# The first loads of a gated mixing kernel laid side by side, and its first two products by turns

## The chip, the cores and the metric

The kernel runs on one core of one Trainium2 chip. The metric is the device time of one execution in microseconds (us), the median over several runs. The engines are TensorE (PE, matrix multiplication, with PEld for its weight loads), VectorE (DVE), ScalarE (ACT), GpSimd (POOL) and SyncE (SP). Here SP issues nearly all loads from HBM, and POOL the stores of intermediate results.

## The reference

One input x of 2048 x 512 goes two ways, and a gate of x mixes the two:

```python
g = sigmoid((x * gate_w).sum(-1))
a = Re(DFT_seq @ (x @ DFT_hid))                     # 2048 x 512
b = (silu(x @ w1) * (x @ w3)) @ w2                  # w1, w3: 512 x 1376, w2: 1376 x 512
out = g * a + (1 - g) * b
```

All of it is float32. The change touches only the start of `x @ w1` and `x @ w3`.

## The kernel before, in words

**Arithmetic.** PE multiplies fp32r operands, a rounded form of float32. To keep float32 accuracy each operand is split into a high part (rounded) and a low part (the rest), and a product takes three matmuls: high times high, low times high, high times low. `high` (line 107) rounds on ACT, `low` (line 110) subtracts on DVE, and `split` does both.

**Blocks.** The products are done by a Strassen-like scheme on 2 x 2 blocks. Of x transposed the blocks are B11, B12, B21 and B22 (each 128 partitions x 1024 columns, 512 KB; a "half" g of 1024 tokens has four of them), and sums of them called T1 to T4 (line 203). The weights w1 and w3 come in 11 chunks of 128 columns; a chunk is 128 x 1024 and holds A11, A12, A22 and A21 with 256 columns each. Seven products make one item, that is one chunk with one half of x.

**Order.** The order of the instructions is the program's own (`manual_schedule`, line 401): every engine runs its instructions in the order in which the code emits them, and waits on semaphores for what it reads and for buffers to come free. The first item (chunk 0, half 0) is written out by hand in lines 402 to 502 and done without the seven-product scheme: eight plain block products into four PSUM tiles, C00, C10, C01, C11, each `half(...)` being six matmuls (two parts r of the contraction, three matmuls each). From line 474 on the usual scheme begins: `prod1` and `prod2` make two products of a chunk ahead (X and Y), and `gate_up(n)` (line 338) does the rest of item n.

**The start.** SP first loads A11 alone (line 402, 128 rows of 1024 bytes), then B11 (line 403, 128 rows of 4096 bytes), then the other three blocks of chunk 0 (line 410, rows of 3072 bytes), then B21, B12, B22, then chunks 1, 2 and 3 (lines 411 to 415). DVE clears a tile `warm` (line 405), and PE multiplies it WARM = 11 times by itself in bf16 (lines 407 and 408), whose results nobody reads. Then come A11's split, B11's split in pieces (lines 444 to 447), the product C00 of A11 with B11, A21's split and the product C10 of A21 with B11, and so on. Chunk 4's load (line 461) reuses the place of chunk 0.

**Places.** The four x blocks lie in F32 places `F4`, of which there are four at that time; T2, T3 and T4 are written over B11, B12 and B21 (lines 466, 494, 501). At line 509 the four places are freed, and the blocks of half 1 are loaded into them. The split parts of half 1 have a large tile of their own in pool `xo1`, written only from item 2 on.

Of the kernel before, what the change touches and what calls it, by code (L numbers as in the profile page):

```python
# [7 lines left out]
F32 = mybir.dt.float32  # L8
F32R = mybir.dt.float32r
# [3 lines left out]
P = 128  # L13
# [4 lines left out]
TB = 512  # L18
# [5 lines left out]
NP2 = (NC + 1) // 2  # L24
WARM = 11
LOOK = 3
# [6 lines left out]
def fnet_swiglu_gate_kernel(  # L33
    ctx: ExitStack,
    tc: tile.TileContext,
    xn: bass.AP,
    xt: bass.AP,
    cc: bass.AP,
    dd: bass.AP,
# [67 lines left out]
    def high(hi, src):  # L107
        nc.scalar.activation(hi, src, AF.Copy)  # L108

    def low(hi, lo, src):  # L110
        nc.vector.tensor_sub(lo, src, hi.bitcast(F32))  # L111

    def split(hi, lo, src):
        high(hi, src)
        low(hi, lo, src)
# [79 lines left out]
    def load_xo(g, k):  # L195

        if g not in XO:
            XO[g] = (xo1 if g else xo0).tile([P, 2, 7, 2, 512], F32R, tag="xo", name=f"xo{g}")
        ST[g, k] = wide(f"xs{g}_{k}")
        nc.sync.dma_start(ST[g, k], xt[g, XRAW.index(k)])  # L200
# [20 lines left out]
    def load_w(w, lo=0, hi=4):  # L221
        if lo == 0:
            WS[w] = f4_a.tile([P, 4, 256], F32, tag=f"f4_{4 + w % (LOOK + 1)}", name=f"ws{w}")
        nc.sync.dma_start(WS[w][:, lo:hi].rearrange("p a n -> p (a n)"),  # L224
                          w13[SETS[w], :, lo * 256 : hi * 256])
# [7 lines left out]
    def wa_parts(w, lo, hi):  # L233
        return (*(flat(WA[w][:, h, lo:hi]) for h in range(2)), flat(WS[w][:, lo:hi]))
# [166 lines left out]
    ctx.enter_context(tc.manual_schedule())  # L401
    load_w(0, 0, 1)
    load_xo(0, "B11")
    warm = s1p.tile([P, 1024], mybir.dt.bfloat16, tag="s1", name="warm")[:, :512]
    nc.vector.memset(warm, 0.0)
    wps = bank(7, "wps")
    for n in range(WARM):
        nc.tensor.matmul(wps, warm[:, :P], warm, start=True, stop=True)
    nc.scalar.activation(act0, warm[:, :24], AF.Silu)
    load_w(0, 1, 4)  # L410
    for k in ("B21", "B12", "B22"):
        load_xo(0, k)
# [8 lines left out]

    def half(i, j, w, x, start):


        wp = lambda h, sl: a21[:, h, sl] if w is None else WA[0][:, h, w, sl]
        xp = lambda q, h: b12[:, h, q * 512 : (q + 1) * 512] if x is None else XO[0][:, h, x, q, :]
        for r in range(2):
            sl = slice(r * P, (r + 1) * P)
            for n, (u, v) in enumerate(((0, 0), (1, 0), (0, 1))):
                nc.tensor.matmul(C[i, j], wp(u, sl), xp(r, v), start=start and r == n == 0,  # L430
                                 stop=not start and r == 1 and n == 2)
# [9 lines left out]
    new_wa(0)  # L441
    split(*wa_parts(0, 0, 1))

    hi, lo, src = xo_half("B11", 0)
    high(hi[:, :256], src[:, :256])
    nc.vector.tensor_copy(hi[:, 256:], src[:, 256:])
    low(hi, lo, src)
    split(*xo_half("B11", 1))
    half(0, 0, 0, 0, True)
    split(a21[:, 0], a21[:, 1], WS[0][:, 3])  # L450
    half(1, 0, None, 0, True)
    split(*wa_parts(0, 1, 3))
    for q in range(2):
        split(*xo_half("B21", q))
    half(0, 0, 1, 1, False)
# [4 lines left out]
    half(0, 1, 0, None, True)  # L460
    WS.pop(0)
    load_w(4)
    sum_xo(0, "T1", t1)
    half(1, 1, None, None, True)
    nc.vector.tensor_mul(h0[:, :512], s1, C[1, 0])
    store_h(0, 0, h0[:, :512])
    sum_xo(0, "T2", ST[0, "B11"])
    half(0, 1, 1, 2, False)
    for w in (1, 2):
        new_wa(w)  # L470
        split(*wa_parts(w, 0, 3))
    half(1, 1, 2, 2, False)
# [35 lines left out]
    do(ahead, 1, lambda: split_xo(0, "T4"))  # L508
    do(second, 1, free, *(ST[0, b] for b in ("B11", "B21", "B12", "B22")))
    do(second, 1, sum_g, 2, y2)  # L510
# [505 lines left out]
```

## Time and profile before

| what | us |
|---|---|
| median of 3 runs | 709.98 (709.84 to 710.0) |
| the profiled execution | 710.08 |
| its span in the profile | 708.3 |
| PE busy in the span | 702.8 |
| DVE busy | 605.1 |
| ACT busy | 369.4 |

The profile is of one execution. The span runs from its first to its last instruction in the trace; the rest of its time lies outside of that. In the rows below, times are from the span's start. A row of the timeline gives the start, the duration, the engine, the line, the operation, what is written and read, how many instructions are merged in it and, in brackets, the idle time ahead of it with what ended it. A row of the groups gives the busy time and the mean duration in ns, and behind the next bar the idle time ahead of the group's instructions. A row of the DMA issues ends with the time from issue to landing. Durations of matmuls overlap, so the distance from one start to the next is their real cost.

### The profile page before, as it was taken

How to read it: one execution, taken by the hardware profiler on the slowest of the kernel's cores; microseconds unless marked ns; L12 is line 12 of the kernel's file. 1: busy time of each engine (PE TensorE's matmuls, PEld its weight loads, DVE VectorE, ACT ScalarE, POOL GpSimd, SP SyncE). 2: the span in 40 equal slices, each digit the busy share in tenths (PEclk: the TensorE clock that was granted, in tenths of full speed). 3: DMA queues.
4: the chain of work that ended last, by engine and by line, in shares of the span. 5: the costliest groups of instructions: out<-in, count | busy, mean ns of one | idle time of the engine just before them, and what ended most of it. 6: DMA issues, size and time to landing. Idle time of an engine off the chain costs nothing.

```text
span 708.3 us, 8597 instructions
## 1 busy us (share of the span) xinstructions
PE 702.8 (99%) x3089; PEld 578.6 (82%) x3089; DVE 605.1 (85%) x735; ACT 369.4 (52%) x479; POOL 64.0 (9%) x118
## 2 busy tenths in 40 slices
PE   9999999999999999999999999999999999999997
PEld 6888888888888888888888888888888888888886
DVE  7989988787679999877999589969997896898985
ACT  6666555655446754454554553544455455455451
POOL 0011111211110000000110001100110000000000
PEclk9999999999999999999999999999999999999999
DMA  7676546499997566712596238914999971773932
GB/s 281 222 270 231 214 183 255 178 319 356 417 412 270 212 210 233 282 60 89 179 358 250 90 129 298 359 60 179 384 418 415 356 274 54 298 281 139 321 120 89
DMA packets 45403, 172.54 MB, mean 244 GB/s; under 512 B 5296, under 2 KB 5424, under 8 KB 41520
## 3 DMA queue, kind: packets, MB, share of 16 engines
q1 hardware_dynamic: 32464, 118.50, 45.6%
q0 software_dynamic: 12608, 52.97, 18.8%
q8 instruction: 24, 0.39, 0.2%
q10 hardware_dynamic: 288, 0.52, 0.2%
q14 instruction: 19, 0.16, 0.1%
HBM read 114.82 MB, written 57.16 MB: 243 GB/s over the span
## 4 chain that ended last, share of the span: by engine, by line
PE 99%; DMA 1%; DVE 0%; ACT 0%; SPq 0%; issue 0%
PE P L119 69%; PE X L119 16%; PE Z L119 8%; PE Y L119 4%; PE C L430 2%; DMA xs_B<-xt 1%; DVE zc L809 0%; ACT xo L108 0%; SPq L224 0%
## 5 line engine op out<-in xcount | busy, mean ns | idle before, releaser
L119 PE MATMUL P<-zo,a 128*128 128x512 f32 x1344 | 305.5, 389 | 0.0
L119 PEld LDWEIGHTS P<-zo,a 128*128 128x128 f32 x1344 | 252.0, 188 | 53.4 <-DVE zo L111 1.1
L108 ACT ACTIVATE zo<-B 128x1024 fp32r<-128x1024 f32 (+1 forms) x182 | 189.2, 1045 | 184.5 <-PE P L119 96.9
L111 DVE TENSOR_TENSOR zo<-B,zo 128x1024 fp32r<-128x1024 f32 (+1 forms) x182 | 217.4, 1202 | 48.3 <-ACT zo L108 47.5
L119 PE MATMUL P<-zo,H 128*128 128x512 f32 x468 | 106.2, 389 | 0.0
L119 PEld LDWEIGHTS P<-zo,H 128*128 128x128 f32 x468 | 87.8, 188 | 18.2
L667 DVE TENSOR_TENSOR B<-B,B 128x1024 f32<-128x1024 f32 (+1 forms) x78 | 92.7, 1188 | 0.1
L119 PE MATMUL X<-xo,wb 128*128 128x512 f32 x378 | 92.7, 389 | 0.0
L119 PEld LDWEIGHTS X<-xo,wb 128*128 128x128 f32 x378 | 70.9, 188 | 14.7
L119 PE MATMUL P<-zo,Y 128*128 128x512 f32 x336 | 76.3, 389 | 0.0
L119 PEld LDWEIGHTS P<-zo,Y 128*128 128x128 f32 x336 | 63.1, 188 | 13.1
L327 POOL DMA_DIRECT2D hsp<-h x42 | 23.0, 548 | 127.4 <-DVE h L381 75.4
L119 PE MATMUL X<-xo,wa 128*128 128x512 f32 x126 | 32.0, 389 | 0.0
L119 PE MATMUL Y<-xo,wa 128*128 128x512 f32 x126 | 32.0, 389 | 0.0
L119 PE MATMUL Z<-xo,wb 128*128 128x512 f32 x126 | 32.0, 389 | 0.0
L119 PE MATMUL Z<-xo,wa 128*128 128x512 f32 x126 | 32.0, 389 | 0.0
L670 DVE TENSOR_TENSOR B<-B,B 128x1024 f32<-128x1024 f32 x26 | 31.6, 1217 | 0.0
L884 ACT ACTIVATE zu<-P 128x512 f32<-128x512 f32 x32 | 19.1, 598 | 20.3 <-PE P L119 20.3
L375 DVE TENSOR_TENSOR u<-u,X 128x512 f32<-128x512 f32 x21 | 14.4, 687 | 15.9 <-PE X L119 15.9
L119 PEld LDWEIGHTS Y<-xo,wa 128*128 128x128 f32 x126 | 23.6, 188 | 4.9
L119 PEld LDWEIGHTS X<-xo,wa 128*128 128x128 f32 x126 | 23.6, 188 | 4.9
L119 PEld LDWEIGHTS Z<-xo,wa 128*128 128x128 f32 x126 | 23.6, 188 | 4.9
(135 smaller groups left out, 549.6 us busy)
## 6 DMA issues: line engine op xcount, KB each, us to landing
B<-cc SPq DMA_DIRECT2D x64, 512.0 KB, 6.0
hsp<-h POOLq DMA_DIRECT2D x42, 256.0 KB, 3.6
B<-hsp SPq DMA_DIRECT2D x20, 512.0 KB, 10.4
wbsp<-wb POOLq DMA_DIRECT2D x8, 1024.0 KB, 4.2
wb<-wbsp SPq DMA_DIRECT2D x8, 1024.0 KB, 8.0
B<-zsp SPq DMA_DIRECT2D x16, 512.0 KB, 7.7
H<-w2sp SPq DMA_DIRECT2D x6, 1024.0 KB, 9.4
ws<-w SPq DMA_DIRECT2D x11, 512.0 KB, 4.4
```

The source lines that it names most:

```text
L108: nc.scalar.activation(hi, src, AF.Copy)
L111: nc.vector.tensor_sub(lo, src, hi.bitcast(F32))
L119: nc.tensor.matmul(ps, u, v, start=first and n == 0, stop=last and n == 2, skip_group_check=chain)
L327: nc.gpsimd.dma_start(hsp[g, b + k, j // 2, :, j % 2 * 512 : (j % 2 + 1) * 512], h)
L375: nc.vector.tensor_add(u4, u4, x)
L430: nc.tensor.matmul(C[i, j], wp(u, sl), xp(r, v), start=start and r == n == 0, stop=not start and r == 1 and n == 2)
L667: nc.vector.tensor_add(t, t, RAW[blk, b, q][:, :n])
L670: nc.vector.tensor_sub(t, RAW[blk, "B12", q], t)
L884: nc.scalar.activation(U[name][:, r], ps[r], AF.Copy)
```

## The change

The host lays out one more input, `first`, of three rows of 128 x 1024: [A11, A21, left half of B11], [right half of B11, left half of B21], [right half of B21, A12, A22]. A left or right half has 512 columns. The kernel loads the three with one DMA each, all with rows of 4096 bytes, into the place of the tile that later holds half 1's split parts; B11 and B21 are views of it, and T2 and T4 are written there too. Chunk 0 has no load of its own any more. The warm-up multiplies a constant tile of ones that the program's preamble sets, 9 times instead of 11, and DVE's clearing goes. The left half of B11 is rounded by DVE in one cast of 512 columns (before: half by ACT, half by DVE). The two products of B11 are done by turns, so that each matmul comes about when its split part does; A12 and A22 are split apart, between the halves of B21; chunk 1 is split ahead of the sum T2. Chunk 4's load doesn't wait for chunk 0's place. F4's places are used by two x blocks instead of four, and so the loads of B11 and B21 of half 1 have places that were never used.

```diff
-WARM = 11
+WARM = 9
...
-    load_w(0, 0, 1)
-    load_xo(0, "B11")
-    warm = s1p.tile([P, 1024], mybir.dt.bfloat16, tag="s1", name="warm")[:, :512]
-    nc.vector.memset(warm, 0.0)
+    tf = xo1.tile([P, 2, 7, 2, 512], F32, tag="xo", name="first")
+    tf = tf.rearrange("p h o q n -> p (h o q n)")[:, : 3 * 1024]
+    XO[0] = xo0.tile([P, 2, 7, 2, 512], F32R, tag="xo", name="xo0")
+    for i in range(3):
+        nc.sync.dma_start(tf[:, i * 1024 : (i + 1) * 1024], first[i])
+    ST[0, "B11"], ST[0, "B21"] = tf[:, 512:1536], tf[:, 1536:2560]
+    RAW0 = {k: tf[:, n : n + 256] for k, n in (("A11", 0), ("A21", 256), ("A12", 2560), ("A22", 2816))}
+    warm = nc.const_aps.tensor(1.0, [P, 512], mybir.dt.bfloat16)
...
-    load_w(0, 1, 4)
-    for k in ("B21", "B12", "B22"):
+    for k in ("B12", "B22"):
         load_xo(0, k)
...
-    def half(i, j, w, x, start):
+    def half(i, j, w, x, start, some=None):
...
+                if some is not None and (r, n) not in some:
+                    continue
...
-    split(*wa_parts(0, 0, 1))
+    w_parts = lambda i, k: (WA[0][:, 0, i], WA[0][:, 1, i], RAW0[k])
     hi, lo, src = xo_half("B11", 0)
-    high(hi[:, :256], src[:, :256])
-    nc.vector.tensor_copy(hi[:, 256:], src[:, 256:])
+    nc.vector.tensor_copy(hi, src)
+    split(*w_parts(0, "A11"))
     low(hi, lo, src)
+    split(a21[:, 0], a21[:, 1], RAW0["A21"])
     split(*xo_half("B11", 1))
-    half(0, 0, 0, 0, True)
-    split(a21[:, 0], a21[:, 1], WS[0][:, 3])
-    half(1, 0, None, 0, True)
-    split(*wa_parts(0, 1, 3))
-    for q in range(2):
-        split(*xo_half("B21", q))
+    for i, some in ((0, ((0, 0), (0, 1))), (1, ((0, 0),)), (0, ((0, 2),)), (1, ((0, 1), (0, 2))),
+                    (0, ((1, 0), (1, 1))), (1, ((1, 0), (1, 1))), (0, ((1, 2),)), (1, ((1, 2),))):
+        half(i, 0, None if i else 0, 0, True, some)
+    split(*xo_half("B21", 0))
+    split(*w_parts(1, "A12"))
+    split(*xo_half("B21", 1))
+    split(*w_parts(2, "A22"))
     half(0, 0, 1, 1, False)
...
-    WS.pop(0)
     load_w(4)
...
+    new_wa(1)
+    split(*wa_parts(1, 0, 3))
     sum_xo(0, "T2", ST[0, "B11"])
     half(0, 1, 1, 2, False)
-    for w in (1, 2):
-        new_wa(w)
-        split(*wa_parts(w, 0, 3))
+    new_wa(2)
+    split(*wa_parts(2, 0, 3))
     half(1, 1, 2, 2, False)
...
-    do(second, 1, free, *(ST[0, b] for b in ("B11", "B21", "B12", "B22")))
+    do(second, 1, free, *(ST[0, b] for b in ("B12", "B22")))
...
+    a11, a12, a22, a21 = arrays["w13"][0].reshape(P, 4, 2 * P).transpose(1, 0, 2)
+    v = np.concatenate([a11, a21, arrays["xt"][0, 1], arrays["xt"][0, 2], a12, a22], 1)
+    arrays["first"] = v.reshape(P, 3, 2 * TB).transpose(1, 0, 2)
```

In the pairs (r, n) of the new loop, r is the part of the contraction (0 takes the left half of B11, 1 the right) and n the matmul of the three: 0 high times high, 1 weights' low part times x's high part, 2 weights' high part times x's low part.

More of the change, by code (lines that the diff above doesn't have):

```diff
@@ L37, in fnet_swiglu_gate_kernel @@
     xt: bass.AP,
+    first: bass.AP,
     cc: bass.AP,
@@ L998 @@
         "xt": np.stack(xq, 1).reshape(2, 4, P, 2 * TB),
+        "first": None,
         "cc": np.stack(cb, 1).reshape(NTB, 4, NG // 2, P, 2 * TB),
```

## The prediction

> **What bounds the kernel now.** I read the page first, then the groups by line for PE, then the chain of waits of the first 8 us, then the timeline and the DMA issues of the first 40 us.
>
> ```profile
> span 708.3 us, 8597 instructions
> ...
> PE 702.8 (99%) x3089; PEld 578.6 (82%) x3089; DVE 605.1 (85%) x735; ACT 369.4 (52%) x479; POOL 64.0 (9%) x118
> ...
> PE 99%; DMA 1%; DVE 0%; ACT 0%; SPq 0%; issue 0%
> ```
>
> TensorE (PE in the rows; DVE is VectorE, ACT ScalarE, SP the engine that issues the loads) is the bound and the chain that ends last is 99% PE. The groups by line, with idle time in the last column:
>
> ```profile
> L119 PE MATMUL P<-zo,a 128*128 128x512 f32 x1344 | 305.5, 389 | 0.0
> ```
>
> Every matmul group from line 119 has 0.0 idle like this first one: once the stream runs it doesn't stop. So the change can save only what lies before it: the first real matmul may start sooner, and the first groups may wait less. The first 8 us of the chain, and PE's first rows:
>
> ```profile
> 1.19 3.93 DMA xs_B<-xt
> ...
> 5.15 0.42 ACT xo L108
> ...
> 5.62 2.38 PE C L430 x8
> ```
> ```profile
> 0.74 0.40 SPq L224 DMA_DIRECT2D ws<-w  x1
> 0.86 0.27 DVE L405 MEMSET warm<- 128x256 uint32 x1 [0.86 <-PEq L1006]
> 1.19 3.89 PE L408 MATMUL wps<-warm 128*128 128x512 bf16 x11 [1.19 <-DVE warm L405]
> 5.62 1.92 PE L430 MATMUL C<-xo,wa 128*128 128x512 f32 x6 [0.54 <-ACT xo L108]
> 8.76 2.88 PE L430 MATMUL C<-xo,wa 128*128 128x512 f32 x12
> 11.48 1.52 PE L430 MATMUL C<-b,wa 128*128 128x512 f32 x6
> ```
>
> B11 lands at 1.19 + 3.93 = 5.12, ACT rounds its first piece, and the first real matmul starts at 5.62; PE stood idle 0.54 us after the warm-ups. The 12 matmuls from 8.76 to 11.48 take 2.72 us, a pitch of 0.227 us. The first 12 (the two products of B11) take 8.76 - 5.62 = 3.14, so 0.42 us more than 2.72, in waits for splits. What the change does not touch follows as it is, moved as a whole.
>
> **The change, part by part.**
>
> *First load.* Before, SP issues A11 (128 KB) at 0.74, B11 (512 KB) at 1.19, the rest of chunk 0 (384 KB) at 1.66, then B21, B12, B22. After, the first issue at 0.74 is a 512 KB load that holds A11, A21 and the left half of B11, and two more such loads follow. When does it land? SP's issues in the timeline, and the time from issue to landing, the rows in the order A11, B11, and then the four of the timeline rows:
>
> ```profile
> 2.13 0.43 SPq L200 DMA_DIRECT2D xs_B<-xt  x1
> ...
> 3.08 0.46 SPq L200 DMA_DIRECT2D xs_B<-xt  x1
> ...
> 27.51 0.33 SPq L200 DMA_DIRECT2D xs_B<-xt  x1
> ...
> 29.82 0.33 SPq L200 DMA_DIRECT2D xs_B<-xt  x1
> ```
> ```profile
> ws<-w SPq DMA_DIRECT2D x1, 128.0 KB, 2.4
> ...
> xs_B<-xt SPq DMA_DIRECT2D x1, 512.0 KB, 3.9
> ...
> xs_B<-xt SPq DMA_DIRECT2D x1, 512.0 KB, 5.2
> ...
> xs_B<-xt SPq DMA_DIRECT2D x1, 512.0 KB, 6.8
> ...
> xs_B<-xt SPq DMA_DIRECT2D x1, 512.0 KB, 3.3
> ...
> xs_B<-xt SPq DMA_DIRECT2D x1, 512.0 KB, 3.2
> ```
>
> B21 landed at 2.13 + 5.2 = 7.33 and B22 at 3.08 + 6.8 = 9.88, with B12 between, so 1.27 us for each 512 KB once the queue is full (413 GB/s). The last two are loads of the second half, of the same shape, that found nothing of SP's queue ahead of them: 3.3 and 3.2 us. B11's 3.9 has A11 ahead. From below: 0.74 + 3.2 = 3.94. From A11: 2.4 us for 128 KB plus 384 KB at 413 GB/s (0.95 us) is 3.35, landing at 4.09. From above, B11's 3.93: landing at 4.67. I take **4.10**, nearest to A11's own row at the same time with nothing ahead. It compares with 5.12. The other two loads follow at 1.27 us each: 5.4 and 6.6. B22 stands behind the same 2560 KB as before, so it gains only the idle stretch around A11: I take 9.4 against 9.88.
>
> *From landing to the first matmul.* The splits, by shape:
>
> ```profile
> L111 DVE TENSOR_TENSOR xo<-xs_B,xo 128x512 fp32r<-128x512 f32 x4 | 2.6, 688 | 0.4 <-ACT xo L108 0.4
> L111 DVE TENSOR_TENSOR a<-ws,a 128x256 fp32r<-128x256 f32 x1 | 0.4, 418 | 0.0
> L446 DVE CAST xo<-xs_B 128x256 fp32r<-128x256 f32 x1 | 0.3, 295 | 1.1 <-DMA xs_B<-xt 1.1
> ```
> ```profile
> L108 ACT ACTIVATE xo<-xs_B 128x512 fp32r<-128x512 f32 x3 | 1.8, 621 | 0.3 <-DMA xs_B<-xt 0.3
> L108 ACT ACTIVATE xo<-xs_B 128x1024 fp32r<-128x1024 f32 x4 | 4.2, 1062 | 2.7 <-DVE xs_B L207 2.4 <-DMA xs_B<-xt 0.2
> ```
>
> The first matmul needs A11's high part (ACT, 0.42, as before) and the high part of all 512 columns of B11's left half, now one DVE cast. A cast of 512 columns isn't in the trace: at least 0.295 (the 256 cast), at most 0.59 (twice it). I take 0.44, about ACT's 0.42, so it costs at most 0.17 more. First matmul at 4.10 + 0.03 + 0.44 + 0.05 = **4.62**, which is 1.00 earlier than 5.62.
>
> *Two products by turns.* PE's order is C00 twice, C10, C00, C10 twice, then likewise for the right half; DVE's is cast, A11 low (256), B11 left low (512), A21 low (256), B11 right low (512). In the trace DVE starts of 256 lie 0.33 apart, of 512 0.60. A11 low ends 5.02, so matmul 2 is at 5.07 (0.22 late); matmul 3 at 5.30; B11 left low ends 5.61, matmul 4 at 5.66 (0.13 late); A21 low ends 5.95, matmul 5 at 6.00 (0.11 late). Matmul 7, due 6.45, needs the right half's high part: 5.4 + 0.62 + 0.08 = 6.1, in time. Matmul 11, due 7.36, needs its low part: 6.8. So the 12th ends its turn at 7.81, 3.19 us after 4.62: the waits are 0.47 where they were 0.42, which **loses 0.05**. The B21 products want A12 low at about 8.0; A12 lands at 6.6, and ACT 0.42 and DVE's queue put it at 7.7. In time.
>
> *Warm-ups.* The memset (0.27) goes, so PE starts about 0.86 instead of 1.19, and 9 remain instead of 11.
>
> ```profile
> 2.02 0.15 PEld L408 LDWEIGHTS <-warm 128*128 128x128 bf16 x1 [0.28 <-issue]
> 2.45 0.15 PEld L408 LDWEIGHTS <-warm 128*128 128x128 bf16 x1 [0.28 <-issue]
> ...
> 4.06 0.53 PEld L408 LDWEIGHTS <-warm 128*128 128x128 bf16 x3 [0.18 <-issue]
> ```
>
> Their pitch was 0.43 us until about 4.1 and half of that after: full rate came 2.9 us after the first one. Nine from 0.86 end between 4.4 (rate doubles at 4.1) and 4.7 (it doesn't): by 4.62 or 0.08 late. I cost them at nothing. [...]
>
> *Vector queue behind it.* DVE becomes the question, since it is full there:
>
> ```profile
> 12.00:14.00 2.00, 2.00 (x11) 1.65 (x10) 2.00 (x4) 1.08 (x2) 0.00 (x0) 1.00 0.98 401
> ...
> 20.00:25.00 5.00, 5.00 (x24) 4.14 (x23) 5.00 (x6) 3.77 (x6) 1.09 (x2) 1.00 0.46 161
> ```
>
> The third time of a row is DVE: 2.00 of 2 us and 5.00 of 5 us, and the two stretches between the rows are as full. What opens this, and what PE waits for behind it:
>
> ```profile
> 11.04 1.23 DVE L111 TENSOR_TENSOR xo<-xs_B,xo 128x1024 fp32r<-128x1024 f32 x1
> ...
> 16.79 1.22 DVE L111 TENSOR_TENSOR xo<-xs_B,xo 128x1024 fp32r<-128x1024 f32 x1
> ...
> 25.35 0.96 DVE L111 TENSOR_TENSOR wa<-ws,wa 128x768 fp32r<-128x768 f32 x1 [0.33 <-ACT wa L108]
> 32.99 1.23 DVE L111 TENSOR_TENSOR wb<-wu,wb 128x1024 fp32r<-128x1024 f32 x1 [0.53 <-ACT wb L108]
> 33.24 2.88 PE L119 MATMUL X<-xo,wb 128*128 128x512 f32 x12
> 36.05 0.95 DVE L111 TENSOR_TENSOR wa<-ws,wa 128x768 fp32r<-128x768 f32 x1
> 37.32 1.52 PE L119 MATMUL X<-xo,wa 128*128 128x512 f32 x6
> ```
>
> The first row, B22's low part, waits for B22 (9.88) and ACT's 1.06; with B22 at 9.4 it starts at 10.55, 0.5 earlier and not 0.95. The second row, T2's low part, is 5.75 us behind the first. After the change the low part of chunk 1 stands ahead of the sum T2 and no longer behind it, where the low parts of chunks 1 and 2 covered ACT's rounding of T2 (1.06): 10.55, then T1 (1.15), h0 (1.13), chunk 1 (0.6 + 0.9) and T2 (1.2) end at 15.55, ACT at 16.64, and T2's low part starts at 16.68, only 0.1 earlier. At 33.24 the seventh matmul (34.60) starts chunk 2's second set; its second (34.83) needs the low part that ends 34.22: 0.6 us to spare. At 37.32 the second (37.55) needs what ends 37.00: 0.55 to spare. PE moves up 0.95. DVE moves up 0.1 at T2's low part and, since the 0.33 us wait at 25.35 is for an ACT step that follows PE, gets back to 0.3 to 0.5 from there. So these two spots are short by 0.95 - 0.4 - 0.55 = 0 to 0.1. I take **0.10 lost**. Behind 40 us PE needs 8.16 us for the 36 matmuls of an item, and DVE, busy 85% of the span, needs less, so DVE gains ground and nothing more is lost.
>
> *Hidden edits.* Chunk 4's load has a place of its own and isn't held until chunk 0 is split; the second half's B11 and B21 go to places never used, so SP issues them about 8 us sooner (19.5 instead of 27.51). They queue behind what PE needs first; nothing on PE waits for them in the trace, cost 0. Two fewer DMA issues on SP, cost 0. POOL's stores follow their producers.
>
> **Sum:** -1.00 + 0.05 + 0.10 = -0.85 us. The profiled execution's own time is 710.08 (span 708.3 plus 1.8 around it), 0.1 above the median 709.98 of the runs; that gives 709.2 for a profile and **709.1** for the median.
>
> **Rivals.**
> 1. *The first load lands as late as B11 does* (3.93 after issue, 4.67), because the load is cold and long. For: A11 needed 2.4 for a quarter of the bytes. Against: the 3.2 and 3.3 rows. First matmul at 5.19: gain 0.43, less 0.05: 709.6. Also the case in which the change doesn't do what it says: the rows are longer, the data no sooner. Chance 0.16.
> 2. *DVE takes over as the limit at 33 to 37 us.* If DVE doesn't move up at all there, PE's 0.95 meets 0.55 of slack: 0.4 lost, gain 0.55, 709.4. For: DVE full and the gap at T2. Against: the 0.33 wait that goes. Chance 0.14.
> 3. *Slower: the clock isn't at full rate when the real matmuls start.* If the gap between warm-ups and first matmul, or their smaller number, makes PE earn it anew (2.9 us from 4.62), 2.9 us of matmuls run at 0.43 instead of 0.227: 1.36 lost, which with -0.85 gives 710.5. [...] Against: before, the 0.54 us gap cost nothing, and the rate doubled during the eighth warm-up. Chance 0.06.
> 4. *More gain*: landing at 3.94 or sooner and no loss behind: 708.8, and with waits among the first 12 also gone 708.4. Chance 0.09.
>
> **How the numbers follow.** The forecast has 0.55, with a range of its own of 708.8 to 709.4. A measurement of this kernel can tell about 0.2% from no change: 1.42 us, so 708.56 and 711.40 are the bounds. The forecast and the first two rivals lie within. Faster by more needs most of rival 4's upper end: 0.07. Slower by more needs rival 3 at worse than its price: 0.03. Within: 0.90. The range runs from the better part of rival 4, 708.5, to beyond rival 1, 709.9; the slow rival is left out.
>
> **What would show it.** Right: the first real matmul at 4.6, the first load landing at 4.1, 12 matmuls in 3.2 us, line 119's groups with idle at or under 0.1, the rest of the span equal. Wrong: landing at 4.5 or later; matmuls at a pitch of 0.43 after 4.6; PE waiting on a DVE split between 16 and 40 us by more than 0.2; any wait on the second half's x.

## The result, and the profile after

| what | before | after |
|---|---|---|
| median | 710.05 us (709.84 to 710.32, 15 runs) | 711.8 us (709.98 to 712.46, 15 runs) |
| the profiled execution | 710.08 | 710.75 |
| its span | 708.3 | 709.0 |

The ratio is 1.0022, 95% interval 1.0014 to 1.003: slower by about 0.2%, where 709.1 us and a gain were forecast. The spread has grown with the median, from 0.5 to 2.5 us. The profiled execution is one of the faster ones, 1.05 us under the median, so it shows only part of the loss; the profiles of the experiments show more of it.

The page of the changed kernel:

```profile
span 709.0 us, 8589 instructions
...
PE 703.5 (99%) x3087; PEld 578.6 (82%) x3087; DVE 605.3 (85%) x735; ACT 368.5 (52%) x479; POOL 63.9 (9%) x118
...
PE 98%; DMA 1%; SPq 0%; DVE 0%; ACT 0%; issue 0%
```

Hardly a digit differs. What happened is in three places of under 2 us each, so the timeline has to be read place by place. Line numbers are those of the changed kernel, one above those of before in the helpers (L120 was L119).

**The start.** The timeline of the changed kernel, first 18 us:

```profile
3.94 0.42 ACT L109 ACTIVATE wa<-first 128x256 fp32r<-128x256 f32 x1 [1.69 <-DMA first<-first]
3.94 0.43 DVE L453 CAST xo<-first 128x512 fp32r<-128x512 f32 x1 [3.94 <-DMA first<-first]
4.39 0.43 DVE L112 TENSOR_TENSOR wa<-first,wa 128x256 fp32r<-128x256 f32 x1
4.52 1.13 PE L438 MATMUL C<-xo,wa 128*128 128x512 f32 x2
5.49 0.39 PE L438 MATMUL C<-xo,a 128*128 128x512 f32 x1
5.49 1.16 ACT L109 ACTIVATE xo<-first 128x512 fp32r<-128x512 f32 x2 [0.83 <-DMA first<-first]
...
7.55 0.39 PE L438 MATMUL C<-xo,a 128*128 128x512 f32 x1
7.90 0.42 ACT L109 ACTIVATE wa<-first 128x256 fp32r<-128x256 f32 x1 [1.25 <-DMA first<-first]
8.37 3.23 PE L438 MATMUL C<-xo,wa 128*128 128x512 f32 x12 [0.43 <-ACT wa L109]
11.44 1.52 PE L438 MATMUL C<-b,wa 128*128 128x512 f32 x6
16.88 1.52 PE L120 MATMUL X<-xo,wa 128*128 128x512 f32 x6
```

The first load lands at 3.94, the second at 5.48 (ACT takes it up at 5.49), and the first real matmul starts at 4.52, 1.10 us before the 5.62 of before. The twelfth starts at 7.55, so the 13th is due at 7.55 + 0.23 = 7.78, a lead of 8.76 - 7.78 = 0.98. It starts at 8.37, and the 12 matmuls from there take 11.44 - 8.37 = 3.07 instead of 2.72. At 11.44 the lead is 0.04 (before: 11.48). The chain of waits of the changed kernel names what took it:

```profile
1.65 6.22 DMA first<-first
...
7.90 0.42 ACT wa L109
...
8.37 3.69 PE C L438 x14
```

That is the third load, issued at 1.65 and landed at 7.87; the forecast had it at 6.6. Its row of the DMA issues (the first load's says 3.2), and the stretches of one us with the rate in GB/s in the last column:

```profile
first<-first SPq DMA_DIRECT2D x1, 512.0 KB, 6.2
```
```profile
3.00:4.00 1.00, 1.00 (x4) 0.32 (x3) 0.06 (x1) 0.06 (x1) 0.00 (x0) 1.00 1.02 406
4.00:5.00 1.00, 1.00 (x3) 0.42 (x2) 0.98 (x3) 0.66 (x2) 0.00 (x0) 1.00 0.95 311
5.00:6.00 1.00, 1.00 (x5) 0.80 (x5) 0.75 (x2) 0.51 (x1) 0.00 (x0) 1.00 0.85 279
```

The rate falls to 279 GB/s between 5 and 6 us, just when the third load is under way (381 in the next microsecond), where the kernel before had 410 and the forecast counted on 413.

**The store behind the loads.** Tile h has two buffers, and item 1's h (written by ACT in line 363) takes the buffer of h0, whose second half POOL stores with `hsp<-h`. The timeline, and the DMA issue of that store:

```profile
20.39 0.33 SPq L225 DMA_DIRECT2D ws<-w  x1
20.76 5.97 SPq L201 DMA_DIRECT2D xs_B<-xt  x4
21.23 0.55 POOL L328 DMA_DIRECT2D hsp<-h  x1 [5.72 <-DVE h L494]
27.77 0.60 ACT L363 ACTIVATE h<-X 128x512 f32<-128x512 f32 x1 [1.95 <-DMA hsp<-h]
```
```profile
hsp<-h POOLq DMA_DIRECT2D x1, 256.0 KB, 6.4
```
In the kernel before the same two views had:

```profile
20.38 0.55 POOL L327 DMA_DIRECT2D hsp<-h  x1 [5.37 <-DVE h L483]
26.64 0.60 ACT L362 ACTIVATE h<-X 128x512 f32<-128x512 f32 x1 [1.32 <-PE X L119]
```
```profile
hsp<-h POOLq DMA_DIRECT2D x1, 256.0 KB, 3.3
```

SP now issues chunk 5's weights at 20.39 and the second half's x right behind, at 20.76; the store comes at 21.23, lands after 6.4 us instead of 3.3, at 27.63, and ACT waits for it until 27.77. ACT's rounding, DVE's low parts and PE stand behind that. PE's rows further on:

```profile
27.76 1.52 PE L120 MATMUL X<-xo,wa 128*128 128x512 f32 x6
37.52 1.53 PE L120 MATMUL X<-xo,wa 128*128 128x512 f32 x6
42.96 2.88 PE L120 MATMUL X<-xo,wb 128*128 128x512 f32 x12
```

Before, the second of these came at 37.32, and the first and third at 27.80 and 42.76. So 0.24 us is lost between 28 and 37, and PE goes on 0.20 behind the kernel before. PE's rows here have no idle time in brackets: a wait under the 0.16 us by which a matmul of 0.39 reaches over the next one's start at 0.23 isn't counted. Only the distances between starts show it.

**The last store.** The last subtraction and the store of its result, changed kernel:

```profile
704.77 0.69 DVE L820 TENSOR_TENSOR zc<-P,nb 128x512 f32<-128x512 f32 x1 [1.72 <-PE P L120]
```
```profile
out<-zc ACTq DMA_DIRECT2D x1, 256.0 KB, 2.5
```

And before:

```profile
704.60 0.69 DVE L809 TENSOR_TENSOR zc<-P,nb 128x512 f32<-128x512 f32 x1 [1.73 <-PE P L119]
```
```profile
out<-zc ACTq DMA_DIRECT2D x1, 256.0 KB, 2.0
```

0.17 us from PE's stream and 0.5 us from the store itself, which the change doesn't touch: 0.67, and 710.75 - 710.08 = 0.67.

### The profile page after: what moved, and what is told of

It is laid out like the page before. It is cut to its first block, busy times and chain, and to the rows that moved or that the text cites. A ratio compares the mean times of both kernels' runs of the same rounds, so it can differ in the third digit from the quotient of the medians.

```text
span 709.0 us, 8589 instructions
## 1 busy us (share of the span) xinstructions
PE 703.5 (99%) x3087; PEld 578.6 (82%) x3087; DVE 605.3 (85%) x735; ACT 368.5 (52%) x479; POOL 63.9 (9%) x118
## 4 chain that ended last, share of the span: by engine, by line
PE 98%; DMA 1%; SPq 0%; DVE 0%; ACT 0%; issue 0%
PE P L120 69%; PE X L120 16%; PE Z L120 8%; PE Y L120 4%; PE C L438 1%; DMA first<-first 1%; SPq L409 0%; DVE zc L820 0%; ACT wa L109 0%
## 5 line engine op out<-in xcount | busy, mean ns | idle before, releaser
L120 PE MATMUL P<-zo,a 128*128 128x512 f32 x1344 | 305.4, 389 | 0.0
L120 PEld LDWEIGHTS P<-zo,a 128*128 128x128 f32 x1344 | 252.0, 188 | 53.3 <-DVE zo L112 1.1
L120 PE MATMUL P<-zo,H 128*128 128x512 f32 x468 | 106.2, 389 | 0.0
L120 PEld LDWEIGHTS P<-zo,H 128*128 128x128 f32 x468 | 87.8, 188 | 18.2
L120 PE MATMUL X<-xo,wb 128*128 128x512 f32 x378 | 92.8, 389 | 0.0
L120 PEld LDWEIGHTS X<-xo,wb 128*128 128x128 f32 x378 | 70.9, 188 | 15.0 <-DVE u L376 0.3
L120 PE MATMUL P<-zo,Y 128*128 128x512 f32 x336 | 76.3, 389 | 0.0
L120 PEld LDWEIGHTS P<-zo,Y 128*128 128x128 f32 x336 | 63.1, 188 | 13.1
L120 PE MATMUL Z<-xo,wa 128*128 128x512 f32 x126 | 32.0, 389 | 0.0
L120 PE MATMUL Y<-xo,wa 128*128 128x512 f32 x126 | 32.0, 389 | 0.0
L120 PE MATMUL X<-xo,wa 128*128 128x512 f32 x126 | 32.0, 389 | 0.0
L120 PE MATMUL Z<-xo,wb 128*128 128x512 f32 x126 | 32.0, 389 | 0.0
L120 PEld LDWEIGHTS Z<-xo,wa 128*128 128x128 f32 x126 | 23.6, 188 | 5.0 <-DVE xo L112 0.2
L120 PEld LDWEIGHTS Y<-xo,wa 128*128 128x128 f32 x126 | 23.7, 188 | 4.9
L120 PEld LDWEIGHTS Z<-xo,wb 128*128 128x128 f32 x126 | 23.7, 188 | 4.9
```

Source lines behind the costliest of these rows:

```text
L120: nc.tensor.matmul(ps, u, v, start=first and n == 0, stop=last and n == 2, skip_group_check=chain)
```

## The experiments

The theories, with the letters that the expectations use. **A**: the third load lands late and takes the lead back. **B**: nine warm-ups leave PE at half rate in some runs (0.43 us a matmul instead of 0.227). **C**: chunk 1's split ahead of the sum T2 delays DVE. **D**: the second half's early loads delay the store of h. **E**: the new input tensor delays the last store. Each kernel was timed beside the kernel before; kernels of one group share its runs, whose median was 710.25, 710.22, 710.38, 710.26 and 710.26 us in the five groups.

### First group: A, B and C one by one

**Third load not waited for** (on the changed kernel; the first item reads data of the first two loads in its place, so this kernel leaves out part of the computation):

```diff
-    w_parts = lambda i, k: (WA[0][:, 0, i], WA[0][:, 1, i], RAW0[k])
+    w_parts = lambda i, k: (WA[0][:, 0, i], WA[0][:, 1, i], RAW0[{"A12": "A11", "A22": "A21"}.get(k, k)])
...
-    split(*xo_half("B21", 1))
+    split(*xo_half("B21", 1)[:2], xo_half("B21", 0)[2])
```

> The third load is issued as in the changed kernel, but the first item reads the columns of the first two loads in its place (A12, A22 and the right half of B21 are replaced by A11, A21 and the left half of B21, so these products are not the reference's). Theory A (the third load, which lands at 7.87 us in the profile of the changed kernel, late and at a time that differs from run to run, holds PE): the median falls by 0.6 to 1.5 us from 711.8 to 710.3 to 711.2, and the spread of 2.5 us shrinks. Theory B (the clock reaches full rate only after the real matmuls begin, at a time that differs from run to run): the median stays at 711.5 or above with the same spread. Theory C (the vector queue, with chunk 1 ahead of T2, holds PE at 30 to 36 us): PE's early gain is there at 11 us and is gone at 38 us; median 710 to 711.5.

Measured: 711.72 us (711.14 to 712.25), ratio 1.0022 (1.0013 to 1.0031), the profiled execution 711.52. The timeline:

```profile
16.20 1.52 PE L120 MATMUL X<-xo,wa 128*128 128x512 f32 x6
28.45 0.60 ACT L363 ACTIVATE h<-X 128x512 f32<-128x512 f32 x1 [3.10 <-DMA hsp<-h]
29.10 1.66 PE L120 MATMUL X<-xo,wb 128*128 128x512 f32 x6 [0.47 <-ACT h L363]
43.71 2.65 PE L120 MATMUL X<-xo,wb 128*128 128x512 f32 x11
```

A is true as far as it goes: at 16.20 PE is 0.72 us ahead of the kernel before (16.92), where the changed kernel is 0.04 ahead, so the third load costs 0.68. But the median doesn't move. The store of h now takes 7.6 us, ACT waits 3.10 us for it, PE idles 0.47 us at 29.10 behind ACT, and at 43.71 it is 0.95 behind before (42.76): 1.67 lost in one place. A lead gained ahead of the collision is eaten in it, because ACT is let go when the store lands and not when PE is ready. This row is what made D a theory.

**Chunk 1 behind T2 again**:

```diff
-    new_wa(1)
-    split(*wa_parts(1, 0, 3))
     sum_xo(0, "T2", ST[0, "B11"])
     half(0, 1, 1, 2, False)
-    new_wa(2)
-    split(*wa_parts(2, 0, 3))
+    for w in (1, 2):
+        new_wa(w)
+        split(*wa_parts(w, 0, 3))
```

> The changed kernel with chunk 1 split behind the sum T2, as before. Theory C: VectorE loses no 0.35 us at T2, the waits of 0.21 us at 30 to 36 us go, median 0.2 to 0.5 us under 711.8. Theories A and B: no difference beyond 0.2 us.

Measured: 710.96 us (709.78 to 712.19), ratio 1.0012 (1.0003 to 1.002). 0.8 us better in the median, with as wide a spread (2.4 us). The store takes 6.7 us and ACT waits 2.15 us for it. So C probably has a part, of a size that these scattered runs don't settle (the fourth experiment, which leaves the work alone, lies 0.5 under the changed kernel too), but it isn't what scatters the runs.

**The warm-up alone, on the kernel before** (nine of ones, no clearing):

```diff
-WARM = 11
+WARM = 9
...
-    warm = s1p.tile([P, 1024], mybir.dt.bfloat16, tag="s1", name="warm")[:, :512]
-    nc.vector.memset(warm, 0.0)
+    warm = nc.const_aps.tensor(1.0, [P, 512], mybir.dt.bfloat16)
```

> The kernel before with nothing changed but the warm-up: a constant of ones, 9 times, no memset. Its real matmuls start at about 5.62 as before. Theory B: if the clock is late in some runs, the median rises by 0.1 to 0.5 and the spread over 0.5 us. Theories A and C: 710.0, spread 0.5 as before.

Measured: 710.66 us (709.83 to 712.2), ratio 1.0008 (0.9999 to 1.0017). Five of the 11 runs lie at 709.83 to 710.23, and four at 711.06 to 712.2, where none of the kernel before was in this group (its highest of 33: 710.95; of all its 153 runs one lies there, at 711.49, in the second group). The profiled execution (710.03) is one of the good ones, so what the others lose isn't seen there. In it the store of h took 5.0 us (3.3 before), which ACT doesn't feel yet; a later store in other runs is a second possible cause of the tail.

**The rows of the new input in another order** (the third load's data in the first row, and so on):

```diff
-        nc.sync.dma_start(tf[:, i * 1024 : (i + 1) * 1024], first[i])
+        nc.sync.dma_start(tf[:, i * 1024 : (i + 1) * 1024], first[(2, 0, 1)[i]])
...
-    arrays["first"] = v.reshape(P, 3, 2 * TB).transpose(1, 0, 2)
+    arrays["first"] = v.reshape(P, 3, 2 * TB).transpose(1, 0, 2)[[1, 2, 0]]
```

> The changed kernel with the three rows of the new input in another order in memory: the first load reads the last row, the second the first, the third the second. Theory A with the place in memory as the cause (the third row is slow to read): the first load lands late instead of the third, at 5 or later instead of 3.94. Theory A with the place in the queue as the cause: the third load stays the late one, median 711.8 within 0.4.

Measured: 711.28 us (710.07 to 712.47), ratio 1.0016 (1.0007 to 1.0024). The loads land 3.4, 4.4 and 6.0 us after issue: the third one issued is still the late one, so it isn't a row's place in the input that makes it late.

### Second group: D, and where the warm-up hurts

**The second half's loads held as before.** The free places are sorted, so that the loads take those first that have just been freed:

```diff
+    do(at_end, 1, lambda: F4.sort(key=lambda at: at[1]))
```

> The changed kernel, but the loads of the second half's x take the places in order, so that the first waits for T3's split as the loads before waited for T4. Theory D (these loads, issued at 20.8 us instead of 27.5, stand ahead of the store of h0 on the DMA engines; it lands 6.4 to 7.6 us after its issue instead of 3.3, and ScalarE's first write into h1, which takes the same buffer, waits 1.9 to 3.1 us for it): the store lands within 4.5 us, that wait goes, PE has no hole at 28 to 33 us, and the median falls by 0.5 to 1.2 us, to 710.6 to 711.3. Theory A (the third load): no change, 711.5 or above.

Measured: 710.68 us (710.51 to 711.09), ratio 1.0006 (0.9997 to 1.0015): 1.1 us better than the changed kernel, and the spread falls from 2.5 to 0.6 us. The timeline and the issue of the store:

```profile
25.98 3.27 SPq L201 DMA_DIRECT2D xs_B<-xt  x4
...
26.68 0.60 ACT L363 ACTIVATE h<-X 128x512 f32<-128x512 f32 x1 [0.77 <-PE X L120]
```
```profile
hsp<-h POOLq DMA_DIRECT2D x1, 256.0 KB, 3.3
```

One line of code moves the loads from 20.76 to 25.98; the store is back at 3.3 us, and ACT waits for PE as it did before. D holds.

**Chunk 1 behind T2 and 11 warm-ups as well** (the edits of the second and the fifth experiment, and WARM = 11):

> The changed kernel with the loads of the second half held, chunk 1 behind T2 as before, and 11 warm-ups of ones instead of 9. Theories B and D together: 709.4 to 710.0 and a spread under 1 us. Theory D alone: as the run with the loads held, less 0.3. If 11 warm-ups hold PE up (they end as late as 5.5 when the clock stays at half rate): 0.3 to 0.8 more.

Measured: 710.47 us (709.85 to 711.07), ratio 1.0001 (0.9992 to 1.0009). PE's last product ends 0.14 ahead of the kernel before (last subtraction at 704.46), the last store still takes 2.5 us.

**Eleven of ones, on the kernel before** (the third experiment's edit with WARM = 11):

> The kernel before with the constant of ones and no memset, but 11 warm-ups; they start at 0.78 and end at 5.5 at the latest, so there is no hole ahead of the first real matmul. Theory B, that 9 leave PE idle for up to 0.9 us and so the clock late in some runs: median 710.0 to 710.2, no run over 711. The rival, that the ones or the early start do it: some runs over 711, median 710.4 to 710.8, as with 9.

Measured: 710.08 us (709.87 to 710.44), ratio 0.9996 (0.9987 to 1.0005), no tail. So neither the ones nor the earlier start hurt; what is left is the two warm-ups fewer, and the gap that they leave ahead of the real work. It rests on four runs of 11 against none.

**The early loads alone, on the kernel before** (B11 and B21 of chunk 0 in the tile that the change uses, nothing else):

```diff
+    def load_first(i, k):
...
-    load_xo(0, "B11")
+    load_first(0, "B11")
...
-    for k in ("B21", "B12", "B22"):
+    load_first(1, "B21")
+    for k in ("B12", "B22"):
...
-    do(second, 1, free, *(ST[0, b] for b in ("B11", "B21", "B12", "B22")))
+    do(second, 1, free, *(ST[0, b] for b in ("B12", "B22")))
```

> The kernel before with B11 and B21 of the first half loaded into the place of the second half's split parts, so that the second half's first two loads have free places and are issued at about 20 us. Loads at the start, warm-up and order of the products as before. Theory D: the store of h0 lands 6 us or more after its issue, ScalarE waits for it, and the median rises by 0.3 to 1.5 us over 710.1. Theories A and B: 710.1 within 0.2.

Measured: 711.13 us (710.28 to 711.56), ratio 1.001 (1.0001 to 1.0019): 0.9 us lost with no other part of the change. The timeline:

```profile
20.62 6.63 SPq L200 DMA_DIRECT2D xs_B<-xt  x4
...
27.64 0.60 ACT L362 ACTIVATE h<-X 128x512 f32<-128x512 f32 x1 [1.87 <-DMA hsp<-h]
```
The store takes 6.4 us, and the wait is the same to a tenth as in the changed kernel. Part of this run's profiled loss lies earlier: its B21 landed at 8.03 instead of 7.33. Its last store takes 2.0 us.

### Third group: E, and the clock

**The rows written over old data** instead of a new input (with the three edits of the sixth experiment). The third row lies over chunk 0 of the weights, which the second half reads again, so chunk 0's products there are of other data:

```diff
-        nc.sync.dma_start(tf[:, i * 1024 : (i + 1) * 1024], first[i])
+        nc.sync.dma_start(tf[:, i * 1024 : (i + 1) * 1024], (xt[0, 1], xt[0, 2], w13[0])[i])
...
+    arrays["xt"][0, 1], arrays["xt"][0, 2], arrays["w13"][0] = v
```

> The run with the loads held, chunk 1 behind T2 and 11 warm-ups, but with no new input tensor: the host writes the three rows over chunk 0 of the weights and over B11 and B21 in the inputs that are there, which nothing else reads. Theory E (in all six profiles of kernels with the new input the last store of the output takes 2.5 us to land, in all four without it 2.0): the last store lands in 2.0 again and the median falls by 0.5, from 710.47 to 709.9 to 710.1. Rival (the store's 0.5 us has another cause in these kernels): 2.5 and 710.4.

Measured: 709.87 us (709.71 to 710.27), ratio 0.9994 (0.9985 to 1.0003). The last store takes 2.0 us again. The loads land at 4.64, 5.88 and 7.05, evenly, though the first one 0.70 later than in the changed kernel.

**The same, third load not waited for** (nine warm-ups; the first item reads data of the first two loads in its place, as in the first experiment):

> As the run before (but with 9 warm-ups), and nobody of the first item waits for the third load; A12, A22 and the right half of B21 are replaced by data of the first two loads, so these products are not the reference's. If the third load, the collision, the place of chunk 1 and the last store are all that ate the gain: PE keeps its lead of 0.7 us to the end, 709.2 to 709.5. If VectorE or another wait still holds PE behind 20 us: 709.7 or above.

Measured: 709.76 us (709.58 to 710.13), ratio 0.9992 (0.9983 to 1.0). PE's first product X comes at 16.35, 0.57 ahead of the kernel before, and with the collision gone it keeps 0.51 of that to the end (last subtraction at 704.09). The first load landed at 4.34, later than was expected.

**An input that nobody reads, on the kernel before**:

```diff
     xt: bass.AP,
+    first: bass.AP,
...
+        "first": np.zeros((3, P, 2 * TB), np.float32),
```

> The kernel before with one more input tensor of 1.5 MB that nothing reads. Theory E: the last store lands in 2.5 us instead of 2.0 and the median rises by 0.5 to 710.6. Rival (not the tensor, but something that the loads or places do): 2.0 and 710.1.

Measured: 710.85 us (710.38 to 711.13), ratio 1.0006 (0.9997 to 1.0015). The interval holds 1, so the median alone doesn't show a loss. The program's instructions are the same as before, and the last store takes 2.5 us. The profiled execution (710.97) shows something else as well. Its first rows of PE:

```profile
1.19 4.88 PE L409 MATMUL wps<-warm 128*128 128x512 bf16 x11 [1.19 <-DVE warm L406]
5.64 2.33 PE L431 MATMUL C<-xo,wa 128*128 128x512 f32 x6
7.81 1.54 PE L431 MATMUL C<-xo,a 128*128 128x512 f32 x6
```

The 11 warm-ups take 4.88 us, where the same 11 took 3.89 before, and the first product takes 7.81 - 5.64 = 2.17 us against 7.37 - 5.62 = 1.75, so 0.42 us are lost. The weight loads of the warm-ups lie 0.43 us apart up to the last one, at 5.01, where the pitch halved at about 4.1 before; the second product's six matmuls take 9.20 - 7.81 = 1.39 us, 0.23 each. So the rate doubled only behind the warm-ups in this execution, and the time at which it does differs between these two executions of the same instructions.

**Five warm-ups of ones, on the kernel before** (WARM = 5):

> The kernel before with 5 warm-ups of ones instead of 11, so that PE is idle for about 2.6 us ahead of the first real matmul. Theory B (PE idle ahead of the first real matmul leaves the clock at half rate): the real matmuls start at 5.5 at a pitch of 0.43 us for up to 3 us, and the median rises by 0.6 to 1.6 us over 710.1. Rival: no difference.

Measured: 711.79 us (710.87 to 712.61), ratio 1.0021 (1.0012 to 1.0029). The timeline:

```profile
0.78 2.29 PE L407 MATMUL wps<-const-bfloat16-1.0 128*128 128x512 bf16 x5 [0.78 <-PEq L1005]
5.60 2.93 PE L429 MATMUL C<-xo,wa 128*128 128x512 f32 x6 [2.53 <-ACT xo L108]
8.33 2.02 PE L429 MATMUL C<-xo,a 128*128 128x512 f32 x6
10.18 2.90 PE L429 MATMUL C<-xo,wa 128*128 128x512 f32 x12
```

After 2.53 us of idle PE the first six matmuls take 8.33 - 5.60 = 2.73 us, 0.455 each, twice the 0.227 of full rate. The next product begins 1.42 us after its time before (10.18 against 8.76). That is the price that the third rival of the prediction had (1.36), met on the kernel before with too few warm-ups. The five end at 0.78 + 2.29 = 3.07, ahead of the 4.1 at which the rate doubled before, so this run shows a full rate that had not been reached yet; whether a gap takes it away again isn't shown.

### Fourth and fifth group: is it the tensor?

**The changed kernel without the new input** (two rows over the x blocks that nothing reads any more, the third as one row more of the weights' input):

```diff
-        nc.sync.dma_start(tf[:, i * 1024 : (i + 1) * 1024], first[i])
+        nc.sync.dma_start(tf[:, i * 1024 : (i + 1) * 1024], (xt[0, 1], xt[0, 2], w13[NC])[i])
...
+    arrays["w13"] = np.concatenate([arrays["w13"], v[2][None]])
```

> The changed kernel, but its three rows lie in the two old inputs (two over the x blocks B11 and B21 that nothing reads any more, the third as one more row of the weights' input), so the program has no new input; nothing else is undone. Theory E (a new input tensor costs 0.5 us at the output's last store, and makes the first loads slower): the last store 2.0 us instead of 2.5, median 711.2 to 711.4, still with a wide spread since the second half's early loads stay and the second store of h still takes 6 to 7.5 us. Theory D alone (the early loads are the whole loss): median 711.8 as in the changed kernel. If the new tensor is also what sets off the collision: under 710.5.

Measured: 711.95 us (711.26 to 712.33), ratio 1.0023 (1.0013 to 1.0032). The last store takes 2.5 us: a miss for E. The profiled execution (712.12) is as slow as the changed kernel's slower half, and shows in full what D does:

```profile
27.64 1.52 PE L119 MATMUL X<-xo,wa 128*128 128x512 f32 x6
29.76 1.66 PE L119 MATMUL X<-xo,wb 128*128 128x512 f32 x6 [0.60 <-ACT h L362]
...
31.96 1.43 PE L119 MATMUL Z<-xo,wa 128*128 128x512 f32 x5 [0.27 <-DVE xo L111]
33.23 1.52 PE L119 MATMUL Y<-xo,wa 128*128 128x512 f32 x6
44.30 1.98 PE L119 MATMUL X<-xo,wb 128*128 128x512 f32 x8
```
```profile
ACT h L362 <- DMA hsp<-h: 3.4, 1, 3.4
```

(The last row is of the waits: 3.4 us in all, once; the store took 7.9.) PE is 0.16 ahead of the kernel before at 27.64 and 1.54 behind at 44.30 (42.76): it waits for ACT's copy that frees its bank, then for the low part that DVE makes from ACT's late rounding.

**All three losses taken back** (this, with the edits of the sixth experiment; nothing of the computation is left out):

> No new input, the second half's loads in their old places, chunk 1 behind T2 and 11 warm-up matmuls of ones; the first loads side by side and the products by turns stay. Nothing of the computation is changed. If the run with the rows in place of old data told the gain of the start rightly: median 709.7 to 709.9, ratio 0.9985 to 0.9995 with a spread of 0.6 us, first real matmul at 5.0 to 5.2, last store 2.0. If its gain came from the overwritten data or from chance: 710.3 to 710.5.

Measured: 710.41 us (710.23 to 710.61), ratio 1.0001 (0.9992 to 1.001). PE is as far ahead at the end as in the ninth experiment (last subtraction at 704.38, there at 704.32), but the last store takes 2.5 us, there 2.0, and that is the whole difference. The two programs differ in one row of 512 KB in an input, and in the data of chunk 0. So it isn't the new tensor; E in that form fell. Nor is PE ahead of the seventh experiment, the kernel before with nothing changed but its 11 warm-ups, whose last subtraction comes at 704.40: with the first load landing at 4.64 here, the new layout of the loads shows no gain of its own.

**A new input declared last, the output first**:

```diff
+    out = nc.dram_tensor("out", (D, S), F32, kind="ExternalOutput").ap()
     args = [
...
-    args.append(nc.dram_tensor("out", (D, S), F32, kind="ExternalOutput").ap())
+    args.append(out)
```

> The run with all three losses taken back, but the three rows are again an input of their own, declared as the last of all tensors, and the output is declared first of all, so that neither the old inputs nor the output move in HBM if places are given in the order of declaration. If the last store's 0.5 us hangs on where the tensors lie in HBM: last store 2.0 us, median 709.7 to 710.0. If it hangs on how many bytes of input the program has, wherever they lie: last store 2.5, median 710.3 to 710.5, as in the run before this one.

Measured: 710.26 us (709.97 to 710.6), ratio 0.9999 (0.999 to 1.0009), last store 2.5 us: a miss for the place of the output, if places go by the order of declaration.

**The new input made 16 MB long** (29 rows of zeros that nobody reads):

```diff
-    arrays["first"] = v.reshape(P, 3, 2 * TB).transpose(1, 0, 2)
+    arrays["first"] = np.zeros((32, P, 2 * TB), np.float32)
+    arrays["first"][:3] = v.reshape(P, 3, 2 * TB).transpose(1, 0, 2)
```

> The same kernel with the three rows at the head of a new input of 16 MB (29 unread rows of zeros behind them), in the place that the changed kernel gives it, so all tensors behind it move by 16 MB instead of 1.5 MB. If the last store hangs on the low bits of the output's place (a move by 16 MB leaves them): last store 2.0 us, median 709.7 to 710.0. If it hangs on the amount of input, or on high bits: 2.5 us or more, median 710.3 or more.

Measured: 710.08 us (709.58 to 710.54), ratio 0.9995 (0.9986 to 1.0004). The last store, with 16 MB of input more:

```profile
out<-zc ACTq DMA_DIRECT2D x1, 256.0 KB, 2.0
```

With all three losses taken back, 0.5 MB more of input (the fourteenth), 1.5 MB more (the fifteenth) and 16 MB more (the last) give 2.5, 2.5 and 2.0 us. So neither a new tensor nor the amount of input sets it. It isn't ACT's queue either: the store of 256 KB that SP issues to the output 2.4 us ahead of the last one takes 3.4 or 3.5 us in seven profiles with a last store of 2.5, and 2.9 us in five with 2.0. That the output's place in HBM sets it, by its lower bits, is no more than a guess, which would fit these rows if places don't go by the order of declaration (the fifteenth); where the tensors were put isn't in the trace, so it is not shown. The medians don't settle it, since the last one lies only 0.18 us under the fifteenth's, within their scatter. Its profiled execution is the longest of its 11 runs (710.54), and in it the third load was late again (6.6 us after its issue, at 8.3).

## Why the prediction was wrong, step by step

- **First load and first matmul: right in the changed kernel.** 3.94 and 4.52, forecast 4.10 and 4.62. In six kernels with the new input the first load landed at 3.94 to 4.34; in the four whose rows lie in old inputs it landed at 4.34 to 4.64, up to the 4.67 of the first rival.
- **Two products by turns: right.** The twelfth matmul starts 3.03 us after the first, so the 12 take 3.26 with one more pitch, forecast 3.19. They do so although the first two took 5.49 - 4.52 = 0.97 us. The second could start when A11's low part was done, at 4.39 + 0.43 = 4.82, so at full rate the third would have come at about 5.1; it came at 5.49. So PE was still at half rate past 5, and not at full rate from 4.1 on, as I had read from the kernel before. (The granted clock in the rows of one us reads 1.00 all the while, so the rate is read from the distance between starts alone.) From 5.49 to 7.55 the starts lie 0.23 us apart, so the full rate was there 4.71 us after the first warm-up at 0.78, where I had taken 2.9 us from one trace. The half rate cost little: at full rate the low parts of B11 (done at 5.41) and of A21 (done at 5.76) would have held the fourth and fifth matmul, and by an estimate from these rows the twelfth would have started at 7.40 instead of 7.55.
- **The other two loads "follow at 1.27 us each: 5.4 and 6.6": wrong for the third.** The second landed at 5.48, the third at 7.87 in the changed kernel, and 5.4 to 6.6 us after its issue in the kernels with three such loads. Not waiting for it brings 0.68 us. In six kernels with the new input it landed 2.1 to 2.8 us behind the second, in the four without 1.2 to 2.0. Why it is late stays open: it isn't the row (fourth experiment), and it came 1.2 and 1.3 us behind the second in the ninth and the fourteenth. B22 was late with it: ACT took it up at 10.44, where 9.4 was forecast (2048 KB stand ahead of it, or 2560 with its own).
- **"Hidden edits ... nothing on PE waits for them in the trace, cost 0": this is the step that failed most, and without it the kernel is level (1.0006, the interval holds 1).** The forecast asked who reads the early loads, and nobody does so early; it didn't ask what other transfers are under way in those microseconds. A 256 KB store of POOL was issued (21.23) behind 512 KB loads of SP (from 20.76 on), its landing frees a buffer of h, and ACT, which waited 1.95 us for it, and DVE and PE behind ACT hang on that buffer. Putting the loads back brings 1.1 us and takes most of the spread away; the early loads alone cost 0.9 on the kernel before. The store took 6.4 to 7.9 us in the six profiles with the early loads, and 3.1 to 3.5 us in ten of the twelve without them. The collision also ate the lead that PE brought to it in the first experiment (0.72 us ahead at 16.20, 0.95 behind at 43.71), so that a gain at the start is worth nothing here as long as these loads come early. How the store is held up, behind the loads or beside them, isn't shown; and it took 5.0 and 5.1 us in the other two without early loads (third and tenth), short of what ACT feels.
- **Vector queue, 0.10 lost: the number holds, its terms don't.** With the loads held (fifth experiment), PE takes 25.91 us from the first product X (16.96) to the product that stands at 42.76 in the kernel before (42.87 here), against 25.84 there, so 0.07 is lost. But PE hadn't moved up by 0.95 there, it was 0.04 behind (16.96 against 16.92). In the changed kernel it was 0.04 ahead (16.88), and T2's low part began not 0.1 earlier but 0.84 later (17.63 against 16.79). Only the distance between the two, 0.88 us where 0.95 - 0.1 = 0.85 was forecast, is the same, with B22 and the third load both late, and that is luck. (An item is also 42 matmuls and 9.52 us, from 33.24 to 42.76, and not 36 and 8.16, which only gives DVE more room.) Where the store is late, chunk 1's place may be worth 0.8 in the median (second experiment against the changed kernel).
- **Warm-ups at no cost: right for the changed kernel, by luck.** The real matmuls come so early there that the gap is small, and with the loads held the runs spread by 0.6 us only. On the kernel before, with its later first matmul, nine leave a tail (third experiment). That the tail is the half rate is argued from the run with five (0.455 us a matmul) and from the late doubling in the eleventh experiment (past 5.01), not seen in a run with nine.
- **The last store: not in the forecast at all.** 0.5 us, in all ten profiles of kernels whose inputs grew by 0.5 or 1.5 MB.

Together: 1.1 (early loads) + 0.5 (last store) + about 0.7 (third load) is 2.3 of the 2.7 us between 709.1 and 711.8; chunk 1's place is the likeliest for most of the rest. That the three simply add up is argued: where the early loads stay, the third load's 0.68 is eaten. The nearest check is the tenth experiment, where none of them costs anything: PE kept 0.51 us of the forecast 0.85, and its first load landed 0.24 later than forecast. The second rival had the right stretch (33 to 37 us), and its 0.4 us stand against the 0.24 lost in the profiled execution, but it had the wrong cause: DVE was late because ACT was, and ACT because of a store. None of the rivals priced a transfer that is delayed by another.

No version of the change beats the kernel before by more than can be told: the best that leave nothing out are at 0.9995 and 0.9999 of it, with intervals that hold 1, and the kernel before with 11 warm-ups of ones is at 0.9996.

## What to carry to other kernels

A load issued sooner is not free because its reader comes late (loads issued at 20.76 instead of 25.98 cost 1.1 us here): list the transfers, of every issuing engine, that are in flight in those microseconds, and ask which buffer each of them frees. Where a program waits on such a store, time won ahead of it can be lost again there (0.72 us ahead became 0.95 behind in the first experiment), so an edit's gain must be followed past the next wait on a DMA and not only to the point where it arises. And where the runs of a changed kernel scatter more than those of before, look for a race between transfers first; here the spread, which fell from 2.5 to 0.6 us with the loads held, told more than the median when one candidate at a time was undone.

## What the runs showed of the hardware that was not expected

- A last store of 256 KB took 2.0 or 2.5 us, in one profile of each of 18 kernels, by how many bytes of input the program declared: 2.0 in all seven with no more than before, 2.5 in all ten with 0.5 or 1.5 MB more, 2.0 in the one with 16 MB more. The kernel before and the eleventh experiment differ in nothing else.
- Five warm-ups of 2.29 us and 2.53 us without matmuls behind them left the next six at 0.455 us each, twice the usual pitch. And the same 11 warm-ups of the kernel before took 3.89 us in one execution and 4.88 in another (the eleventh experiment).
- Of three equal loads of 512 KB in a row from the start, the third landed 1.2 to 2.8 us after the second in different kernels, at 279 to 381 GB/s between 4 and 7 us in the changed kernel, where 413 had been read from the kernel before.
